# All products of probabilities with 128 columns, on eleven fixed tiles

## The chip, the cores and the metric

The kernel runs on one core of one Trainium2 chip. The metric is the device time of one execution in microseconds (us); it is a median over runs. Beside it stands one execution under the hardware profiler, with its own time and its trace. Engines are named as in the profile: PE (TensorE, matrix products), PEld (its weight loads, which run beside the products), DVE (VectorE), ACT (ScalarE), POOL (GpSimd) and SP (which issues most transfers).

## The reference

Three layers follow one another. First attention with a threshold, over 4 batches, 8 heads, 576 queries and keys and a head size of 64:

```python
scores = scale * np.matmul(q, k.transpose(0, 1, 3, 2))
thresh = np.max(scores, axis=-1, keepdims=True) - tau
scores = np.where(scores >= thresh, scores, -1000000000.0)
scores = scores - np.max(scores, axis=-1, keepdims=True)
attn = np.exp(scores)
attn = attn / (np.sum(attn, axis=-1, keepdims=True) + 1e-09)
return np.matmul(attn, v).astype(np.float32)
```

Its output, with the heads side by side, is a row of 512 values for each of 2304 tokens. Then each token goes through one of 8 experts (512 to 1024 and back, ReLU between); which one comes from the largest of its 8 logits, or from the token before it where a second gate says so. Last come a layer norm, a dense layer 512 to 2048 to 512 with ReLU, and a sum with its input. The change lies in attention.

## The kernel before, in words

**Attention.** The loop `while it < NI or later` goes over items. An item is (p, j): p is one of 16 pairs of heads (two heads of one batch), j one of 9 blocks of keys, in the order 8, 0, 1, ... 7. Blocks 0 to 3 are 128 keys each of the pair's first head, 4 to 7 those of the second, and block 8 has the last 64 keys of both, one head in each half of the partitions. Each turn of the loop works on several items at different stages:

- `s_mm` (PE) makes scores with queries on the partitions, and `mx` (DVE, L403) takes their maximum for each query, one item ahead of `s_mm` of the next. `th_parts` and `th_rows` turn a pair's maxima into rows of thresholds.
- `t_mm` (PE, L436 and L441) makes scores again with keys on the partitions, minus the thresholds; `ex` (ACT, L446) takes the exponential; `mask` (DVE, L452) sets to zero what lies below the threshold and writes tile `em`, of which there are two buffers.
- `hilo` splits the masked probabilities into two halves of 16 bits: ACT copies (L458), POOL subtracts (L459). Both go to a tile of 128 keys by 2 x 576 queries, `hl`, or `hlt` for block 8. `hl` has nine buffers in rotation, `hlt` two.
- `pv` (PE, L474 to L478) multiplies the halves with the values' halves, `vh` and `vl`. The probabilities are the weights (the stationary operand), so the queries are the columns of the array and the rows of the output `o`. A call makes one group of queries t of one head a: t from 0 to 3 has 128 queries, t = 4 has the last 64. It has fifteen products, three for each of five blocks of keys: high with `vh` (65 columns of output, the last one is the sum of the probabilities), high with `vl`, low with `vh`. For t = 4 the first of the three reads 128 columns of the tile all the same, so that all 128 rows of the output are written, and the other two read 64.
- `norm` (DVE, L489 to L493) divides by the sums after t = 4 of a head; then come the transfer to DRAM (`store`) and, from `gate`, transposes and the products for the routing.

Each engine works through its instructions in the order in which the loop issues them; `at` puts a step at a turn. `pv` of a pair's first head runs with its last group at turn 9p + 9, that of the second head at 9p + 13; `norm` follows one turn later, ahead of that turn's `mask`. Within a turn the order is: `mx`, `ex`, `mask`, `hilo`, the next `s_mm`, `pv`, `t_mm`, and then the rest (`gate` and `route` for tokens that are done, loads and splits of q, k and v for pairs to come, and the making of 16-bit halves of the dense layer's weights: `ffn_steps`, L142 to L164).

**Columns.** `columns(a, t)` gives the first column of a group: the first head's queries 0 to 511 are followed by its last 64 at 512, the second head's last 64 stand at column 0 of its tile, ahead of the others.

**After attention.** Experts, two tiles of 128 tokens each and then further tiles by counts; then the dense layer. Weights come in through SP's queue and are split on ACT and DVE. `blanks` writes constants once at the start.

Of the kernel before, what the change touches and what calls it, by code (L numbers as in the profile page):

```python
# [9 lines left out]
F16 = mybir.dt.float16  # L10
I32 = mybir.dt.int32
BF16 = mybir.dt.bfloat16
AF = mybir.ActivationFunctionType
ALU = mybir.AluOpType
# [6 lines left out]
def kernel(  # L21
# [15 lines left out]
    nc = tc.nc  # L37
# [15 lines left out]
    def pool(c, name, bufs, **kw):  # L53
        return c.enter_context(tc.tile_pool(name=name, bufs=bufs, **kw))
# [152 lines left out]
    R = dict(side="right")  # L207
    c_raw, c_tab, c_unit, c_tail, c_cv, c_pv, c_main = (ExitStack() for _ in range(7))
# [8 lines left out]
    cv_p = pool(c_cv, "cv", 2, **R)  # L217
    vb_p = pool(c_pv, "vb", 1, **R)
    sm_p = pool(c_pv, "sm", 2, **R)
    hl_p = pool(c_pv, "hl", 9, **R)  # L220
    ps_v = pool(c_pv, "ps_v", 1, space=PSUM, **R)
    em_p = pool(c_main, "em", 2, **R)
    e_p = pool(c_main, "e", 2, **R)
# [6 lines left out]
    if True:  # L230
# [15 lines left out]
        def blanks():  # L246
            V, G = nc.vector, nc.gpsimd
            for i in range(2):
                vh = vb[i][0]
                V.memset(pts[i], 0.0)  # L250
                G.memset(vh[:, :, 64:65], 16.0)
                G.memset(vh[64:128, 4, 64:65], 0.0)
                G.memset(vh[0:64, 5, 64:65], 0.0)
                V.memset(lgs[i], 0.0)
                V.memset(e1s[i], 0.0)
                V.memset(xts[i][:, 4, 64:128], 0.0)
                V.memset(mcs[i], 0.0)
            V.memset(erow, 0.0)
            V.memset(oh, 0.0)
            V.memset(one1, 1.0)  # L260
            V.tensor_copy(out=identb, in_=ident)
            V.memset(ind, 0.0)
            for i in range(4):
                V.memset(ind[32 * i:32 * i + 3, i, :], 1.0)
# [94 lines left out]
        def split_v(p):  # L359
# [2 lines left out]
            nc.scalar.activation(out=vh[:, :, 0:64], in_=r, func=AF.Copy)  # L362
            nc.gpsimd.tensor_tensor(out=vl, in0=r, in1=vh[:, :, 0:64], op=ALU.subtract)

        mms, mst, hls, ths, pvs, xcs = {}, {}, {}, {}, {}, {}
        W0 = 224
        mm = nc.tensor.matmul
# [11 lines left out]
        def columns(a, t):  # L379

            return 128 * t + 64 * a if t < 4 else 512 * (1 - a)
# [72 lines left out]

        def hilo(p, j):
            em = mst.pop((p, j))
            hl = hl_p.tile([128, 2, 576], F16, name="hlt" if j == 8 else "hl", bufs=2 if j == 8 else 9)
            nc.scalar.activation(out=hl[:, 0], in_=em, func=AF.Copy)  # L458
            nc.gpsimd.tensor_tensor(out=hl[:, 1], in0=em, in1=hl[:, 0], op=ALU.subtract)  # L459
            hls[p, j] = hl  # L460

        def pv(p, a, t):

            vh, vl = vb[p % 2]
            if t == 0:
                pvs[p, a] = ps_v.tile([128, 5, 100], F32, name="o")
            M = 128 if t < 4 else 64
            o, n = pvs[p, a][0:M, t], columns(a, t)
            for c in range(5):
                hl = hls[p, 4 * a + c if c < 4 else 8]  # L470
                jv = (c, 4)[c == 4] if a == 0 else (6 + c, 5)[c == 4]
                hi = hl.rearrange("p a b -> p (a b)")[:, n:n + 128]
                if c < 4:
                    mm(pvs[p, a][:, t, 0:65], hi, vh[:, jv, 0:65], start=(c == 0), stop=False)  # L474
                mm(o[:, 0:64], hl[:, 0, n:n + M], vl[:, jv, :], start=False, stop=False)
                mm(o[:, 0:65], hl[:, 1, n:n + M], vh[:, jv, 0:65], start=False, stop=False)
                if c == 4:
                    mm(pvs[p, a][:, t, 0:65], hi, vh[:, jv, 0:65], start=False, stop=True)  # L478
            if t == 4:
                for c in range(4):  # L480
                    del hls[p, 4 * a + c]
                if a: del hls[p, 8]
# [77 lines left out]
        def route(b):  # L560
# [112 lines left out]
            def f_A(t):  # L673
                for i in range(5):
                    M = 128 if i < 4 else 64
                    for a in range(2):
                        nc.tensor.matmul(t[:, 0:4 * E], ol[0:M, i], ov[0:M, i, 2 * a:2 * a + 2].rearrange("p a b -> p (a b)"), start=(i + a == 0), stop=(i + a == 5))

# [74 lines left out]
        for p in range(npair):  # L753
            if p:
                for lead, f, *a in soon.get(p, prep):
                    at(9 * p - lead, f, p, *a)
                at(9 * p - 4, th_parts, p)
                at(9 * p - 2, th_rows, p)
            for a in range(2):
                for n, ts in enumerate(((0, 1), (2, 3), (4,))):  # L760
                    for t in ts:
                        at(9 * p + 7 + 4 * a + n, pv, p, a, t)
                at(9 * p + 10 + 4 * a, start_norm, p, a)
            at(9 * p + 15 + (4 if p == npair - 2 else 1 if p < npair - 2 else 0), store, p)
            at(9 * p + (17 if p < npair - 1 else 15), lambda p=p: bgp.append(gate(p)))
# [109 lines left out]
    def dyn_tables():  # L875
        A = P["pa"].tile([128, 4, 128], F32, name="a").rearrange("p a b -> p (a b)")[:, 0:2 * NDYN]
        for i in range(B * 5):
            M = 128 if i % 5 < 4 else 64
            for a in range(2):
# [40 lines left out]
    for u in range(E + ND0):  # L920
        fq += [(u, j) for j in range(8)]
        n = 0 if u == 0 else 1
# [262 lines left out]
    with tc.manual_schedule():  # L1185
# [20 lines left out]
        for nm in "qkv":  # L1206
            load(0, nm, 1)
        blanks()
        nc.vector.tensor_scalar(out=ge, in0=t0, scalar1=0.0, scalar2=None, op0=ALU.is_ge)
        nc.vector.tensor_scalar(out=qs, in0=ge, scalar1=16.0, scalar2=None, op0=ALU.mult)  # L1210
# [14 lines left out]
        while it < NI or later:  # L1225
# [13 lines left out]
            if 0 < it <= NI: hilo(*items[it - 1])  # L1239
# [3 lines left out]
            for f, a in todo:  # L1243
                if f in (pv, th_rows): f(*a)
# [3 lines left out]
            for f, a in todo:  # L1248
                if f not in (pv, th_rows, start_norm): f(*a)
# [44 lines left out]
        while bgp:  # L1294
            n = len(bgp)
# [112 lines left out]
```

## Time and profile before

| what | us |
|---|---|
| median of 3 runs | 1051.86 |
| lowest and highest of them | 1051.25, 1055.43 |
| the profiled execution, its own time | 1051.45 |
| its span, first to last instruction | 1049.7 |
| PE busy in the span | 990.2 |
| DVE busy | 652.8 |
| ACT busy | 505.1 |
| POOL busy | 392.8 |

The span lies inside the profiled execution's time. A busy time is a sum over stages with different limits, so the shares of the whole span say little of one stage. Idle time of an engine costs something only where another engine waits for it. The granted clock of PE is 1.00 for full speed; the mean over this span is 0.988.

### The profile page before, as it was taken

What the parts mean: (1) busy time and instruction counts of PE and PEld (TensorE: products, weight loads), DVE (VectorE), ACT (ScalarE), POOL (GpSimd) and SP (SyncE); (2) the same over time, 40 slices, a digit from 0 to 9 for tenths busy, and PEclk for the clock granted to TensorE, in tenths of its full rate; (3) what the DMA queues carried; (4) which work ended last, traced back from release to release, by engine and by line L of the source; (5) the groups of instructions that cost most, each with busy time, mean ns of one, the idle gap of its engine ahead of it and who ended that gap; (6) DMA issues with size and microseconds to landing.
All of it is one profiled execution on the core that took longest, in us unless ns stands there. A gap on an engine that the chain in (4) does not pass through costs nothing. (4 is left out here: it accounts for less than half of the span.)

```text
span 1049.7 us, 23757 instructions
## 1 busy us (share of the span) xinstructions
PE 990.2 (94%) x9946; PEld 728.9 (69%) x9946; DVE 652.8 (62%) x1127; ACT 505.1 (48%) x791; POOL 392.8 (37%) x411
## 2 busy tenths in 40 slices
PE   6899998998999988899999999999999999999995
PEld 3678877787888776676667677594858668567572
DVE  7788888988897777797787777363324133131220
ACT  4688786786777666356566554242212011011010
POOL 3699897797788671334222211101000000000000
PEclk8999999999999999999999999999999999999998
DMA  7556544464442646668889775363111110111100
GB/s 179 138 133 166 132 103 126 112 156 119 113 108 47 166 153 213 214 217 278 268 290 304 239 251 164 105 200 106 38 31 40 52 32 31 54 28 41 31 11 23
DMA packets 122454, 136.83 MB, mean 130 GB/s; under 512 B 65370, under 2 KB 86874, under 8 KB 122336
## 3 DMA queue, kind: packets, MB, share of 16 engines
q1 hardware_dynamic: 98336, 116.43, 38.3%
q0 software_dynamic: 4960, 14.17, 3.7%
q10 hardware_dynamic: 19040, 4.61, 2.1%
q8 instruction: 80, 1.31, 0.5%
q14 instruction: 38, 0.31, 0.1%
HBM read 100.17 MB, written 19.94 MB: 114 GB/s over the span
## 5 line engine op out<-in xcount | busy, mean ns | idle before, releaser
L1144 PE MATMUL a<-nT,fw 128*128 128x256 f16 x1728 | 190.3, 273 | 0.8 <-DVE nT L1113 0.8
L459 POOL TENSOR_TENSOR hl<-em,hl 128x576 f16<-128x576 f32 x128 | 169.5, 1325 | 54.0 <-ACT hl L458 52.8
L1157 PE MATMUL y<-fw,hid 128*128 128x512 f16 x864 | 187.9, 379 | 0.0
L1144 PEld LDWEIGHTS <-fw 128*128 128x128 f16 x1728 | 169.1, 98 | 22.4 <-issue 0.9
L1157 PEld LDWEIGHTS <-hid 128*128 128x128 f16 x864 | 84.6, 98 | 100.4
L1147 ACT ACTIVATE hid<-a 128x512 f16<-128x512 f32 x72 | 42.7, 593 | 213.2 <-PE a L1144 211.3
L125 DVE SCALAR_TENSOR_TENSOR w<-stg,w 128x1024 f16<-128x1024 f32 x112 | 135.2, 1231 | 15.7 <-ACT w L124 14.8
L446 ACT ACTIVATE e<-s,t 128x576 f32<-128x576 f32 x144 | 106.0, 736 | 70.2 <-PE s L441 57.6
L1162 POOL DMA_INDIRECT out_dram<-xf x18 | 19.1, 1059 | 311.8 <-DVE xf L1161 311.8
L1012 PE MATMUL a<-xT,w 128*128 128x128 f16 (+1 forms) x1536 | 121.4, 241 | 1.4 <-DVE w L125 0.9
L1033 PE MATMUL y<-w,hid 128*128 128x512 f16 x528 | 117.8, 379 | 3.0 <-DVE hid L1017 2.7
L1012 PEld LDWEIGHTS <-w 128*128 128x128 f16 x1536 | 112.2, 99 | 11.1 <-DVE w L125 1.0
L403 DVE TENSOR_REDUCE mc<-sm 128x1 f32<-128x576 f32 x138 | 103.6, 751 | 24.7 <-PE sm L399 22.7
L124 ACT ACTIVATE w<-stg 128x1024 f16<-128x1024 f32 x112 | 114.4, 1051 | 6.1 <-DMA stg<-in_moe_w_dram 3.5
L452 DVE SCALAR_TENSOR_TENSOR em<-s,e 128x576 f32<-128x576 f32 x144 | 107.1, 745 | 9.7 <-POOL hl L459 8.5
L1148 DVE SCALAR_TENSOR_TENSOR hid<-a,hid 128x512 f16<-128x512 f32 x72 | 49.6, 688 | 98.9 <-ACT hid L1147 98.9
L1161 DVE SCALAR_TENSOR_TENSOR xf<-y,xf 128x512 f32<-128x512 f32 x18 | 12.5, 692 | 146.8 <-PE y L1157 146.8
L399 PE MATMUL sm<-qkt 128*128 128x288 f16 (+1 forms) x308 | 75.4, 291 | 24.3 <-DVE mc L403 21.4
L458 ACT ACTIVATE hl<-em 128x576 f16<-128x576 f32 x128 | 86.9, 679 | 18.8 <-DVE em L452 18.3
L1033 PEld LDWEIGHTS <-hid 128*128 128x128 f16 x528 | 51.0, 98 | 62.2 <-DVE hid L1017 4.5
L436 PE MATMUL s<-qkt 128*128 128x288 f16 (+1 forms) x320 | 90.2, 290 | 3.8 <-DVE em L452 3.1
L441 PE MATMUL s<-th,ind 128*128 128x128 bf16 (+5 forms) x960 | 91.9, 206 | 0.0
(295 smaller groups left out, 1800.4 us busy)
## 6 DMA issues: line engine op xcount, KB each, us to landing
stg<-in_moe_w_dram SPq DMA_DIRECT2D x112, 512.0 KB
stg<-in_moe_w_ch_dram SPq DMA_DIRECT2D x32, 512.0 KB
ys_d<-stg SPq DMA_DIRECT2D x6, 769.5 KB
xf<-ys_d SPq DMA_DIRECT2D x9, 513.0 KB
x_d<-xc SPq DMA_DIRECT2D x16, 256.0 KB
ku<-qkt SPq DMA_DIRECT2D x28, 144.0 KB
rawq<-in_q_dram SPq DMA_DIRECT2D x7, 512.0 KB
rawk<-in_k_dram SPq DMA_DIRECT2D x7, 512.0 KB
```

The source lines that it names most:

```text
L124: nc.scalar.activation(out=dst[:, 0, n], in_=t, func=AF.Copy, scale=scale)
L125: nc.vector.scalar_tensor_tensor(out=dst[:, 1, n], in0=t, scalar=scale, in1=dst[:, 0, n], op0=ALU.mult, op1=ALU.subtract)
L403: nc.vector.tensor_reduce(out=mcs[p % 2][:, j:j + 1], in_=mms.pop((p, j))[:, W0:W0 + 576], op=ALU.max, axis=AX.X)
L436: mm(o[:, W0 + 288 * c:W0 + 288 * c + 288], (kt, ku)[k][:, n], y, start=(k == 0), stop=False)
L441: mm(o[:, W0 + i:W0 + i + w], ind[:, t % 4, 0:o.shape[0]], y, start=False, stop=(i == of[-1][0]))
L446: nc.scalar.activation(out=e, in_=mst[p, j][:, W0:W0 + 576], func=AF.Exp, bias=t0, scale=SC)
L452: nc.vector.scalar_tensor_tensor(out=em, in0=ps[:, W0:W0 + 576], scalar=0.0, in1=e, op0=ALU.is_ge, op1=ALU.mult)
L459: nc.gpsimd.tensor_tensor(out=hl[:, 1], in0=em, in1=hl[:, 0], op=ALU.subtract)
L1012: nc.tensor.matmul(ps[:, f, :], t1[:, a, c, fc], x[:, h, i:i + N // 128, c, :], start=(n == 0), stop=(n == 11))
L1033: nc.tensor.matmul(ps, hid[:, x, f, 128 * i:128 * i + 128], t2[:, a, f, :], start=(n == 0), stop=(n == 23))
L1144: nc.tensor.matmul(ps[:, f, :], fw1[:, a, c, fc], x[:, h, :, c, :], start=(n == 0), stop=(n == 11))
L1157: nc.tensor.matmul(ps, hid[:, x, f, ts_], fw2[:, a, f, :], start=(n == 0), stop=(n == 47))
```

## The change

For the last 64 queries of a head every product now reads 128 columns of the tile and writes 128 rows of the output. The 64 rows more are not used. For the second head, whose last queries stand at column 0, the columns beside them are the next 64 queries. For the first head they are, in the high half, the first 64 columns of the low half, and in the low half 64 columns of zeros, which the tile gets behind it. For this the tiles are made once, eleven of them, with a row of 2 x 576 + 64 values; POOL writes the zeros at the start. Block (p, j) uses tile (8p + j) mod 9, and block 8 uses tile 9 + p mod 2. In the last block of keys the product of high with `vh` comes first, as in the others.

```diff
-    hl_p = pool(c_pv, "hl", 9, **R)
+    hl_p = pool(c_pv, "hl", 1, **R)
...
+            for hl in hlt:
+                G.memset(hl[:, 1152:1216], 0.0)
...
+        hlt = [hl_p.tile([128, 2 * 576 + 64], F16, name=f"hl{i}") for i in range(11)]
...
-            hl = hl_p.tile([128, 2, 576], F16, name="hlt" if j == 8 else "hl", bufs=2 if j == 8 else 9)
-            nc.scalar.activation(out=hl[:, 0], in_=em, func=AF.Copy)
-            nc.gpsimd.tensor_tensor(out=hl[:, 1], in0=em, in1=hl[:, 0], op=ALU.subtract)
+            hl = hlt[9 + p % 2] if j == 8 else hlt[(8 * p + j) % 9]
+            nc.scalar.activation(out=hl[:, 0:576], in_=em, func=AF.Copy)
+            nc.gpsimd.tensor_tensor(out=hl[:, 576:1152], in0=em, in1=hl[:, 0:576], op=ALU.subtract)
...
-            M = 128 if t < 4 else 64
-            o, n = pvs[p, a][0:M, t], columns(a, t)
+            o, n = pvs[p, a][:, t], columns(a, t)
             for c in range(5):
                 hl = hls[p, 4 * a + c if c < 4 else 8]
                 jv = (c, 4)[c == 4] if a == 0 else (6 + c, 5)[c == 4]
-                hi = hl.rearrange("p a b -> p (a b)")[:, n:n + 128]
-                if c < 4:
-                    mm(pvs[p, a][:, t, 0:65], hi, vh[:, jv, 0:65], start=(c == 0), stop=False)
-                mm(o[:, 0:64], hl[:, 0, n:n + M], vl[:, jv, :], start=False, stop=False)
-                mm(o[:, 0:65], hl[:, 1, n:n + M], vh[:, jv, 0:65], start=False, stop=False)
-                if c == 4:
-                    mm(pvs[p, a][:, t, 0:65], hi, vh[:, jv, 0:65], start=False, stop=True)
+                hi, lo = hl[:, n:n + 128], hl[:, 576 + n:704 + n]
+                mm(o[:, 0:65], hi, vh[:, jv, 0:65], start=(c == 0), stop=False)
+                mm(o[:, 0:64], hi, vl[:, jv, :], start=False, stop=False)
+                mm(o[:, 0:65], lo, vh[:, jv, 0:65], start=False, stop=(c == 4))
```

## Rows read from the trace of the kernel before

**Rows 1.** Busy time by stage (window: length, then each engine, PE's clock, DMA).

```profile
core 0: us, PE busy (x) PEld busy (x) DVE busy (x) ACT busy (x) POOL busy (x), PEclk, DMA share, GB/s
...
47.00:402.00 355.00, 333.14 (x4889) 278.09 (x4886) 302.06 (x543) 265.52 (x447) 285.96 (x276) 1.00 0.49 125
402.00:1049.70 647.70, 625.12 (x4828) 430.39 (x4825) 314.83 (x509) 215.54 (x309) 85.32 (x82) 0.99 0.41 130
```

**Rows 2.** Busy time of single pairs of heads in the loop, same columns.

```profile
87.24:109.33 22.09, 21.58 (x318) 18.05 (x315) 19.40 (x32) 18.22 (x32) 20.11 (x19) 1.00 0.53 133
153.51:180.36 26.85, 22.42 (x322) 18.50 (x319) 23.28 (x48) 18.62 (x33) 19.25 (x19) 1.00 0.47 124
180.36:203.80 23.44, 22.15 (x331) 18.64 (x329) 21.28 (x42) 16.44 (x28) 16.82 (x17) 1.00 0.40 103
247.99:275.64 27.65, 23.56 (x322) 19.47 (x320) 23.18 (x48) 18.33 (x33) 19.16 (x19) 0.94 0.44 120
...
321.14:343.01 21.87, 21.39 (x318) 18.01 (x316) 17.61 (x29) 17.10 (x30) 18.42 (x19) 1.00 0.26 55
```

**Rows 3.** Waits of DVE, 47 to 402 us (in total, times, longest).

```profile
DVE rd L489 <- PE o L478: 23.8, 30, 2.4
DVE mc L403 <- PE sm L399: 14.7, 20, 2.0
DVE em L452 <- POOL hl L459: 8.5, 13, 1.9
```

**Rows 4.** Weight loads of the products of probabilities by shape (busy us, mean ns).

```profile
L474 PEld LDWEIGHTS <-hl 128*128 128x128 f16 x640 | 60.6, 98 | 9.1 <-issue 2.9
...
L475 PEld LDWEIGHTS <-hl 128*64 128x64 f16 x128 | 13.6, 106 | 6.9
```

**Rows 5.** Timeline of PE, a block of 128 queries and what follows (start, duration).

```profile
194.29 0.19 PE L474 MATMUL o<-vh,hl 128*128 128x65 f16 x1
194.32 0.19 PE L475 MATMUL o<-vl,hl 128*128 128x64 f16 x1
...
194.74 0.19 PE L474 MATMUL o<-vh,hl 128*128 128x65 f16 x1
```

**Rows 6.** Timeline of PE, a first head's block of the last 64 queries.

```profile
212.79 0.19 PE L474 MATMUL o<-vh,hl 128*128 128x65 f16 x1
212.92 0.22 PE L475 MATMUL o<-vl,hl 128*64 128x64 f16 x1
...
213.10 0.20 PE L474 MATMUL o<-vh,hl 128*128 128x65 f16 x1
...
214.15 0.29 PE L436 MATMUL s<-qkt 128*128 128x288 f16 x1
```

**Rows 7.** Timeline of DVE at three such blocks (last column: idle before).

```profile
190.91 0.17 DVE L489 TENSOR_SCALAR rd<-o 128x5 f32<-128x5 f32 x1 [0.42 <-PE o L478]
...
201.26 0.16 DVE L489 TENSOR_SCALAR rd<-o 128x5 f32<-128x5 f32 x1 [0.70 <-PE o L478]
...
214.35 0.17 DVE L489 TENSOR_SCALAR rd<-o 128x5 f32<-128x5 f32 x1 [0.60 <-PE o L478]
...
216.42 0.76 DVE L452 SCALAR_TENSOR_TENSOR em<-s,e 128x576 f32<-128x576 f32 x1
```

**Rows 8.** Timeline of POOL, 203 to 219 us.

```profile
203.80 1.29 POOL L459 TENSOR_TENSOR hl<-em,hl 128x576 f16<-128x576 f32 x1 [2.05 <-ACT hl L458]
...
215.11 1.27 POOL L459 TENSOR_TENSOR hl<-em,hl 128x576 f16<-128x576 f32 x1
216.56 1.28 POOL L459 TENSOR_TENSOR hlt<-em,hlt 128x576 f16<-128x576 f32 x1 [0.17 <-ACT hlt L458]
```

**Rows 9.** Timeline of POOL at the start.

```profile
0.74 0.20 POOL masks.py:197 MEMSET ident<- 128x128 f32 x1 [0.29 <-POOLq L1392]
...
1.26 0.14 POOL L251 MEMSET vh<- 128x10 f16 x1
...
9.59 1.27 POOL L306 TENSOR_TENSOR nat<-rawq,nat 128x576 f16<-128x576 f32 x1 [3.37 <-ACT nat L305]
```

**Rows 10.** The instructions of line L146 (min, median and max ns).

```profile
L146 DVE SCALAR_TENSOR_TENSOR cv<-stg,cv x22: 681/692/1659, 41.6 to 327.2; 128x512 int32<-128x512 int32 x22
```

## The prediction

> **What bounds the kernel now.** I read the granted clock and the page's slices first, then busy time by stage, then waits, then the timelines of single blocks. By stage [rows 1]: the attention loop runs from 47 to 402 us with PE busy 333 of 355 us, the experts and the dense layer fill the rest with PE busy 625 of 648 us. The change touches products of the attention loop alone; what follows has no clock of its own, since its loads are issued in program order as buffers come free, so what the loop saves should arrive whole at the end.
>
> Inside the loop a pair of heads takes about 22.1 us where nothing else disturbs it [rows 2] (the row of 87.24; eight pairs look like it, the last of them the row of 321.14): PE 21.58 busy, POOL 20.11, DVE 19.40. PE is nearly full, POOL is only 2 us behind. So it is not enough to count what PE saves; I must see what is late next.
>
> The waits say where PE holds the others up [rows 3]: DVE's largest wait is the first step of the norm, L489, for the last product of probabilities, L478: 23.8 us in 30 waits. The norm follows exactly the block of products for a head's last 64 queries.
>
> **The products.** A block for 128 queries, fifteen products, goes from 194.29 to 194.74: 0.45 us, one product each 0.03 us [rows 5]. The block for the last 64 queries has the same fifteen, ten of them with 64 columns. It goes from 212.79 to 214.15: 1.36 us [rows 6]. The steps inside say why: the first product has 128 columns, the next starts 0.13 us later with 64, and a group of three takes 0.31 us (212.79 to 213.10) where three equal products take 0.09. PE pays at each change between 64 and 128 columns, twice in each group. After the change all fifteen have 128 columns and the block should take the 0.45 us of its neighbours: 0.91 us less. There are 32 such blocks (128 loads of this kind over four a block [rows 4]), so PE gets back 32 x 0.91 = 29.1 us. The bounds for a block are 0 (if the cost came from somewhere else than the change of columns) and 0.91; I take 0.91, as the block of rows 5 is the new block in every respect: same tiles, same columns, same order but for the last three.
>
> Against the change speaks that ten weight loads grow from 64 to 128 columns. In the trace 64 columns took 106 ns and 128 columns 98 [rows 4], so the smaller load buys nothing, and I charge nothing. The Trainium skill (TensorE: Matmul & The Clock Gate, LDWEIGHTS) says that a load's time goes by its columns, 128 ones at 1.2 columns a ns. By that rule ten loads would cost an estimated 53 ns more each, a block would save 0.38 us instead of 0.91, and the sum below would be about 10 us and the time about 1041, at the slow end of my forecast's own range. The durations of this trace do not bear it out, and I give it 0.02 of the forecast's chance.
>
> **What of the 0.91 us reaches the end.** DVE is the engine to follow, because PE's next scores wait for its maxima. In a second head's block DVE has finished a maximum and stands 0.70 us until the norm can start, at 201.26 [rows 7]. With the block 0.91 us shorter this wait is gone and then DVE's own maximum comes last: gain 0.70 us, not 0.91. POOL does not stand in the way there: it stood idle 2.05 us before the step at 203.80 [rows 8]. Behind the norm stand, on DVE, the mask, then the copy on ACT, then POOL's subtraction: all of them come 0.70 us earlier. Fifteen blocks (after the sixteenth, DVE has splits of expert weights ahead of the norm): 15 x 0.70 = 10.5 us.
>
> A first head's block ends differently. DVE waits 0.60 us for the norm, at 214.35 [rows 7], but POOL has been working without a break since 203.80, until the subtraction that ends at 215.11 + 1.27 = 216.38 [rows 8]. The mask at 216.42 [rows 7] needs one of two buffers, and it is that subtraction which frees it. So the 0.60 us turns into a wait for POOL; what remains is the 0.17 us that POOL idles before its next step. In eight pairs it is like that: 8 x 0.17 = 1.4 us. In the other eight POOL is less busy (16.82 of 23.44 us, the row of 180.36 [rows 2]), there the same wait is 0.42 us, at 190.91 [rows 7], and I take it whole: 8 x 0.42 = 3.4 us.
>
> Sum: 10.5 + 1.4 + 3.4 = 15.3 us.
>
> **The tiles and the zeros.** Eleven fixed tiles take the place of eleven rotating buffers with the same order of use: nine for the first kind, two for the other. A buffer comes back after nine tiles, when its last products are at least three steps of the loop old, and in the waits of ACT this copy never waits for PE. I charge nothing; if that cover were gone a copy would wait for one block, 0.45 us. A product of the last 64 queries now reads 64 columns more, the low half's included; the product that leads each group read that far already, so it waits for nothing new. Eleven memsets of 64 values are added on POOL at the start: 0.14 us for 10 values, 0.20 us for 128 [rows 9], so 1.5 to 2.2 us. POOL idles 3.37 us before its first subtraction at 9.59 [rows 9], since ACT's copy is not there; that hides them. Without this cover they would cost at most 2.2 us.
>
> The profiled execution took 1051.45 us, 0.41 below the median of the runs (1051.86), well inside their spread. 1051.45 - 15.3 = 1036.2 us.
>
> **The rivals.** *All of PE's saving comes back.* 1051.45 - 29.1 = 1022.3 us. For it: PE is busy 21.58 of 22.09 us in a pair [rows 2], and the wait for the norm alone is 23.8 us [rows 3]. Against it: DVE's maximum ends 0.70 us before the norm, so nothing can start 0.91 us earlier, and POOL's run bars the first head. Between 1022 and 1031: chance 0.20.
>
> *POOL and DVE get into each other's way and take the gain.* The same DVE step, L146, takes 0.69 us in the median and 1.66 at most [rows 10]; the long ones lie where POOL works without a break. A pair where small DVE steps fall on such a run takes 26.85 us instead of 23.44 [rows 2] (rows of 153.51 and 180.36). With POOL at 20.11 us of a pair of some 21.3, such meetings get likelier. If every one of 14 pairs has one long step more, 14 x 0.97 = 13.6 us are lost again and 1.7 stay: 1049.8 us. Against it: in the eight like pairs POOL and DVE are moved by the same amount, so their meetings stay what they are. Between 1042 and 1051: chance 0.25, half of it above 1046. The Trainium skill (SBUF — State Buffer, Who interferes with whom) says that DVE and GpSimd share one pair of ports, held for a whole instruction, and that the other blocks; the long L146 fit that.
>
> *The clock falls, and it gets slower.* PE has more idle time in each pair, and around 256 us the granted clock fell once after a long idle stretch: the pair of 247.99 had 0.94 and took 27.65 us, its twin of 153.51 had 1.00 and 26.85 [rows 2]. One fall costs 0.80 us. To lose the 15.3 us and 5.3 more, it would have to fall some 26 times, nearly twice in each pair. Chance 0.03: the idle stretches shown follow DVE's long runs, not these blocks, and the change shortens the busy part, it does not lengthen an idle one by more than a few tenths.
>
> That the change does nothing (the 1.36 us not being due to the columns) would leave 1051; I count it in the second rival.
>
> **How the numbers follow.** Forecast, between 1031 and 1042: 0.52; more: 0.20; less: 0.25; slower: 0.03. A measurement of this kernel can tell about 0.5% (5.3 us) from no change, so faster begins below 1046.2: 0.52 + 0.20 + 0.12 = 0.84; same 0.12; slower 0.04. The range goes from 1027 to 1046.5: it leaves out a quarter of the second case, less than half of the third and the slower one, together about 0.19.
>
> **What would show it.** In the changed kernel's trace: no product of probabilities with 64 columns; the block of the last queries at 0.45 us; DVE's wait for it near zero; pairs of 21.2 to 21.4 us in the loop, with POOL's idle time near nothing and DVE waiting for POOL more than the trace of before shows. Pairs of 20.5 us or less would prove the POOL step wrong: then something else than POOL held the first head's block. A block that still takes over 0.6 us would prove the reading of the columns wrong, and long DVE steps in more pairs the second rival right.

## The result, and the profile after

The median of four runs is 1038.94 us after the change (1038.51 to 1040.08) and 1052.34 us before it (four runs, 1051.25 to 1055.43). The ratio is 0.987, with a 95% interval from 0.9857 to 0.9883: 13.4 us less. The forecast was 1036.2 us, 2.7 us below the median and inside its range of 1027 to 1046.5. The profiled execution took 1038.88 us, against 1051.45 before: 12.6 us less where the sum had 15.3.

Windows of the changed kernel: the two stages (the attention loop, then the rest), then a pair of heads that nothing else disturbs, cut where those of [rows 2] are. Columns as in [rows 1].

```profile
47.00:402.00 355.00, 314.70 (x4975) 269.03 (x4970) 315.56 (x567) 273.84 (x457) 288.08 (x275) 0.99 0.52 135
402.00:1037.10 635.10, 615.52 (x4719) 421.79 (x4718) 305.05 (x485) 207.92 (x298) 84.58 (x82) 0.99 0.40 128
106.88:128.07 21.19, 19.85 (x318) 16.99 (x315) 19.38 (x32) 18.29 (x32) 20.36 (x20) 1.00 0.69 163
```

Seven of the eight such pairs now take 20.9 to 21.2 us where most took 22.09 [rows 2]; the other, from 63.81 us, still takes 22.08, with PE waiting 0.9 us for a transfer in it. PE, nearly full before, is idle 1.34 us of the pair shown; POOL has become the busiest engine, idle only 0.83 us of it.

Two pairs did not get shorter: those in which DVE has the later steps of a routing to do. The first of them, cut at the start of the same two masks, so that DVE's instructions are the same in both windows, in the kernel before and in the changed one:

```profile
166.11:188.74 22.63, 22.25 (x324) 18.58 (x324) 18.59 (x41) 17.23 (x30) 17.32 (x19) 1.00 0.40 107
162.11:184.97 22.86, 20.61 (x324) 17.51 (x324) 20.77 (x41) 17.36 (x30) 18.05 (x19) 1.00 0.45 119
```

Its twin went from 23.53 to 23.81 us. PE is relieved, but DVE is busy 2.2 us longer: three small routing steps take 1.22, 1.00 and 0.88 us where they took 0.2 each. The timelines show one of them in the changed kernel, POOL's subtraction beside it, and the same step in the kernel before.

```profile
180.65 1.22 DVE L644 TENSOR_TENSOR rk<-rk,oh 128x40 f32<-128x40 f32 x1
180.54 1.28 POOL L462 TENSOR_TENSOR hl<-em,hl 128x576 f16<-128x576 f32 x1
185.46 0.19 DVE L645 TENSOR_TENSOR rk<-rk,oh 128x40 f32<-128x40 f32 x1
```

Started 0.11 us after the subtraction, the step ends 0.05 us after it.

DVE's waits in the changed kernel, 47 to 402 us (in total, times, longest).

```profile
DVE mc L406 <- PE sm L402: 18.6, 19, 2.1
DVE em L455 <- POOL hl L462: 7.8, 15, 1.4
DVE rd L488 <- PE o L477: 4.9, 3, 2.2
```

The wait for the last product of probabilities has gone from 23.8 us in 30 waits [rows 3] to 4.9 us in 3. Another wait has grown instead: the same view gives for PE's scores waiting for DVE's maxima 25.0 us, against 16.5 before.

PE's timeline in the changed kernel, the block for a second head's last 64 queries and what follows it (start, duration).

```profile
116.51 0.19 PE L475 MATMUL o<-vh,hl 128*128 128x65 f16 x1
116.54 0.20 PE L476 MATMUL o<-vl,hl 128*128 128x64 f16 x1
116.57 0.19 PE L477 MATMUL o<-vh,hl 128*128 128x65 f16 x1
...
116.96 0.29 PE L439 MATMUL s<-qkt 128*128 128x288 f16 x1
```

116.51 to 116.96 is 0.45 us, as in [rows 5] and not the 1.36 us of [rows 6]. The weight loads did not become dearer (groups of loads by shape, whole span; busy us, mean ns):

```profile
L475 PEld LDWEIGHTS <-hl 128*128 128x128 f16 x800 | 74.1, 97 | 5.7 <-issue 2.9 <-DVE xc L492 0.6
```

How much of the time is gained inside the loop, the list of one line's instructions shows. The loop's masks, in the changed kernel:

```profile
L455 DVE SCALAR_TENSOR_TENSOR em<-s,e x144: 729/742/759, 30.2 to 380.4; 128x576 f32<-128x576 f32 x144
```

The last mask starts at 380.4 us, where the same view of the kernel before has 392.5: 12.1 of the 12.6 us are gained up to there.

### The profile page after: what moved, and what is told of

Its sections match the earlier page's. It is cut to its first block, busy times and chain, and to the rows that moved or that the text cites. A ratio compares the mean times of both kernels' runs of the same rounds, so it can differ in the third digit from the quotient of the medians.

```text
span 1037.1 us, 23768 instructions
## 1 busy us (share of the span) xinstructions
PE 962.8 (93%) x9946; PEld 711.7 (69%) x9946; DVE 656.1 (63%) x1127; ACT 506.5 (49%) x791; POOL 396.4 (38%) x422
## 5 line engine op out<-in xcount | busy, mean ns | idle before, releaser
L462 POOL TENSOR_TENSOR hl<-em,hl 128x576 f16<-128x576 f32 x144 | 192.9, 1343 | 56.1 <-ACT hl L461 53.2
L461 ACT ACTIVATE hl<-em 128x576 f16<-128x576 f32 x144 | 97.8, 679 | 23.4 <-DVE em L455 22.8
```

The source lines that it names most:

```text
L461: nc.scalar.activation(out=hl[:, 0:576], in_=em, func=AF.Copy)
L462: nc.gpsimd.tensor_tensor(out=hl[:, 576:1152], in0=em, in1=hl[:, 0:576], op=ALU.subtract)
```

## The experiments

Each kernel ran beside the kernel before on the same chip; a ratio is to that one, with its 95% interval. "A like pair" is a pair of heads that nothing else disturbs, 22.09 us before and mostly 20.9 to 21.2 after.

**Only the tiles and the zeros.** The ten products with 64 columns stay, in the old order.

```diff
+                M = 128 if t < 4 else 64
+                if c < 4:
+                    mm(o[:, 0:65], hi, vh[:, jv, 0:65], start=(c == 0), stop=False)
+                mm(o[0:M, 0:64], hl[:, n:n + M], vl[:, jv, :], start=False, stop=False)
+                mm(o[0:M, 0:65], hl[:, 576 + n:576 + n + M], vh[:, jv, 0:65], start=False, stop=False)
+                if c == 4:
+                    mm(o[:, 0:65], hi, vh[:, jv, 0:65], start=False, stop=True)
```

> The eleven fixed tiles, their zeros and the memsets alone; the products of the last 64 queries keep 64 columns. If the gain comes from the columns: within 2 us of the kernel before, and the blocks of the last queries still take 1.36 us. If part of the gain comes from the fixed tiles (other waits at the copy, the start of the loop 0.6 us earlier): 1 to 6 us faster than before.

1052.11 us against 1052.00, ratio 0.9999 (0.9979 to 1.0019); a like pair takes 22.09 us. Tiles and zeros neither cost nor give anything, as far as an interval of 2 us either way can tell.

**128 columns only for the second heads, or only for the first.** The edit is shown against the kernel with the tiles alone.

```diff
-                M = 128 if t < 4 else 64
+                M = 128 if t < 4 or a == 1 else 64
```

and with `a == 0` in the other kernel.

> 128 columns for the second head's last queries alone, the first head's keep 64. By the forecast's sum this block brings 0.70 us, fifteen times: 10.5 us of the gain, so about 1041 to 1042 us. If PE's time alone counted, half of the whole gain of 13.4 us: 1045 to 1046 us.

> 128 columns for the first head's last queries alone. By the forecast's sum 1.4 + 3.4 = 4.8 us, so about 1047 us, with DVE's wait at the norm of the first head gone and a wait of the mask for POOL in its place. If PE's time alone counted, half of the whole gain: 1045 to 1046 us. If POOL held the block fully: 1050 us or more.

Second heads alone: 1046.01 us, ratio 0.9947 (0.9927 to 0.9967), 5.6 us (3.5 to 7.7) where the forecast's term was 10.5. First heads alone: 1045.96 us, 0.9939 (0.9916 to 0.9963), 6.4 us (3.9 to 8.8) where the terms were 4.8 together. The two add up to 12.0, close to the 13.4 of the whole.

In the kernel with the second heads alone, DVE's waits for the last product (47 to 402 us) fell as foreseen, from 23.8 to 13.1 us: 10.7, where the term says 10.5.

```profile
DVE rd L492 <- PE o L481: 13.1, 17, 2.4
DVE em L455 <- POOL hl L462: 4.1, 5, 1.4
```

But DVE's own work got longer. Its line L146, a step in the making of the dense layer's weights, in the list of that line's instructions (min, median, max ns), in this kernel:

```profile
L146 DVE SCALAR_TENSOR_TENSOR cv<-stg,cv x22: 681/1316/1724, 41.3 to 324.2; 128x512 int32<-128x512 int32 x22
```

The median is 1316 ns, 692 before [rows 10]. Before the change the step began 1.2 us after POOL's step L158, once that was over (at 108.48 and 107.30 us, for one). DVE's timeline of this kernel in one like pair shows it right behind a norm that no longer waits:

```profile
105.53 0.15 DVE L492 TENSOR_SCALAR rd<-o 128x5 f32<-128x5 f32 x1
...
106.87 1.31 DVE L146 SCALAR_TENSOR_TENSOR cv<-stg,cv 128x512 int32<-128x512 int32 x1
```

and POOL's timeline of the same kernel shows what is running beside it, with L158 begun only 0.4 us earlier:

```profile
106.47 1.16 POOL L158 TENSOR_TENSOR fw<-cv,fw 128x512 f16<-128x512 f32 x1
107.59 1.72 POOL L462 TENSOR_TENSOR hl<-em,hl 128x576 f16<-128x576 f32 x1
```

Two of POOL's steps that read memory run during L146, and the second of them takes 1.72 us instead of 1.28. In the busy times by line, 47 to 402 us, DVE's steps L142, L144 and L146 took 58.6 us together before and take 64.3 here, 5.7 more. A like pair takes 21.84 us, though a few take less: 0.25 us gained, not 0.70. In this pair DVE waits 0.7 us less for the last product and 0.4 less for POOL, but it works 0.46 us longer and waits 0.5 longer for PE's scores.

More is lost in the two pairs with the later routing steps. The first of them, cut as above:

```profile
163.98:187.73 23.75, 21.50 (x324) 18.00 (x324) 20.89 (x42) 17.37 (x29) 18.04 (x19) 1.00 0.50 136
```

It took 22.63 us before, its twin 23.53 and now 24.87: 1.1 and 1.3 us lost where 0.70 each had been counted as won. That is 3.9 of the 4.9 us by which the term was too large. The Trainium skill (SBUF — State Buffer, Who interferes with whom) says that a DVE instruction with two inputs in SBUF contends with a GpSimd instruction that reads SBUF; L146 has two inputs and fits that, and so does the routing step on `rk`.

With the first heads alone a like pair takes 21.90 us, 0.19 less, where the forecast had 0.17, and DVE waits more for POOL (8.5 us in 13 waits before [rows 3]):

```profile
DVE em L455 <- POOL hl L462: 12.0, 21, 1.7
```

Here the 0.60 us did turn into a wait for POOL, as the forecast said.

**64 columns kept, but all ten such products in a row.** Two changes of the columns in a block instead of eight: the order of the products before the change gives eight, not the nine of the expectation. `part(c)` gives the tile of block c and the index of its values.

```diff
...
+            if t == 4:
+                for c in range(4):
+                    hl, jv = part(c)
+                    mm(o[:, 0:65], hl[:, n:n + 128], vh[:, jv, 0:65], start=(c == 0), stop=False)
+                for c in range(5):
+                    hl, jv = part(c)
+                    mm(o[0:64, 0:64], hl[:, n:n + 64], vl[:, jv, :], start=False, stop=False)
+                    mm(o[0:64, 0:65], hl[:, 576 + n:640 + n], vh[:, jv, 0:65], start=False, stop=False)
+                hl, jv = part(4)
+                mm(o[:, 0:65], hl[:, n:n + 128], vh[:, jv, 0:65], start=False, stop=True)
...
```

> Fixed tiles, 64 columns kept, but the ten products with 64 columns of a block stand together: two changes of columns in a block and not nine. If the change of columns costs, a block takes 0.65 to 0.75 us and 10 to 13 us come back, about 1040 us. If a product with 64 columns is slow by itself, the block stays above 1.2 us and the time near 1052 us.

1039.49 us, ratio 0.989 (0.9862 to 0.9919), as good as the changed kernel within what can be told. PE's timeline of this kernel, one block:

```profile
115.91 0.29 PE L477 MATMUL o<-vh,hl 128*128 128x65 f16 x4
116.13 0.22 PE L480 MATMUL o<-vl,hl 128*64 128x64 f16 x1
116.19 0.20 PE L481 MATMUL o<-vh,hl 128*64 128x65 f16 x1
116.22 0.20 PE L480 MATMUL o<-vl,hl 128*64 128x64 f16 x1
...
116.44 0.20 PE L481 MATMUL o<-vh,hl 128*64 128x65 f16 x1
116.57 0.20 PE L483 MATMUL o<-vh,hl 128*128 128x65 f16 x1
116.61 0.29 PE L439 MATMUL s<-qkt 128*128 128x288 f16 x1
```

The block takes 0.70 us. Inside the row of ten a product of 64 columns follows the last one after about 0.03 us, like one of 128; only going from 64 back to 128 (116.44 to 116.57) takes 0.13. So what was dear is the change and not the narrow product. With 0.25 us for two changes (0.70 - 0.45), the eight changes of the old block come to 1.0 us; 0.91 was measured, 0.11 each. The Trainium skill (TensorEngine Tiling (Array Packing), Key Properties) says that changing the tiling mode drains TensorE; the trace fits that and puts about 0.1 us on a change, but shows no drain as such.

**The new block three times over.** 45 products of 128 columns take the place of fifteen. The first two passes are computed and thrown away.

```diff
-            for c in range(5):
+            for c in [0, 1, 2, 3, 4] * (3 if t == 4 else 1):
```

> The changed kernel, but the block of the last queries is made three times over, each time anew (same result): 45 products of 128 columns, about 1.36 us, as long as the block before the change, with no change of columns in it. If only the time that PE spends on the block counts: back to 1051 to 1053 us. If the changes of columns also cost outside of the block (later products, other engines): it stays 3 us or more below the kernel before.

1052.39 us, ratio 0.9994 (0.9972 to 1.0017). PE's timeline of this kernel, one such block and what follows:

```profile
106.77 0.20 PE L475 MATMUL o<-vh,hl 128*128 128x65 f16 x1
...
108.11 0.19 PE L477 MATMUL o<-vh,hl 128*128 128x65 f16 x1
108.14 0.29 PE L439 MATMUL s<-qkt 128*128 128x288 f16 x1
```

The block takes 1.37 us, as the old one did, and a window over a like pair is that of [rows 2] again:

```profile
88.87:110.96 22.09, 21.58 (x374) 18.81 (x374) 19.40 (x32) 18.24 (x32) 20.10 (x20) 1.00 0.51 133
```

With PE's time put back and no 64-column product left, the kernel is where it was. So the gain comes from PE's time in these blocks; nothing else of the change gives more than the interval's 2 to 3 us.

**Less work for POOL.** In two more kernels, the one before and the changed one, the low halves of the dense layer's weights are zeros, written by a memset (22 pieces), and not the difference; that part of the output is left out.

```diff
-            nc.gpsimd.tensor_tensor(out=dst[:, 1, a], in0=rf, in1=dst[:, 0, a], op=ALU.subtract)
+            nc.gpsimd.memset(dst[:, 1, a], 0.0)
```

> The kernel before with the same zeros in place of the 22 low halves. There the blocks of the last queries set the pairs as well as POOL, so a lighter POOL should bring little: at most 3 us. If POOL set the pairs of the kernel before already, as much as in the changed kernel: 6 to 12 us.

> The changed kernel, but POOL writes zeros instead of the low halves of the dense layer's weights that it makes inside the attention loop (22 pieces; these low halves are left out). A subtraction of 1.16 us becomes a memset of some 0.3 us, twice in a pair. If POOL's run sets the pairs of the changed kernel: pairs of 20.3 to 20.9 us instead of 21.5, 6 to 12 us faster than the changed kernel. If DVE or PE sets them: at most 2 us.

On the kernel before: 1052.62 us, ratio 0.9994 (0.9978 to 1.0011). On the changed kernel: 1029.39 us, 0.978 (0.9739 to 0.982): 23.6 us below the kernel before, against 13.4 with POOL's work in full. A window over a like pair of the first (before, lighter), columns as in [rows 1]:

```profile
88.59:110.68 22.09, 21.57 (x314) 18.06 (x314) 19.40 (x33) 18.24 (x32) 18.81 (x20) 1.00 0.52 133
```

and of the second (after, lighter):

```profile
95.15:115.79 20.64, 19.85 (x318) 17.00 (x315) 19.25 (x32) 18.14 (x32) 18.86 (x20) 1.00 0.61 121
```

POOL's busy time is the same in both, 18.8 us. Before the change the pair stays at 22.09 with PE full; after it the pair falls to 20.64, though the one right behind it takes 21.47. So POOL holds the changed kernel and did not hold the kernel before.

POOL can hold a kernel by the amount of its work or by its meetings with DVE, and this edit lessens both: a memset takes 0.52 us instead of 1.16, and it reads nothing. In this second kernel the median of L146 is back at 687 ns; at 103.48 us, for one, it takes 0.68, most of it in a gap of 0.62 us in which POOL stands idle. And the first pair with the later routing steps, cut as above, takes

```profile
158.91:179.75 20.84, 20.43 (x324) 17.52 (x324) 18.37 (x41) 16.99 (x30) 16.17 (x18) 1.00 0.42 115
```

where the changed kernel has 22.86. POOL was idle 4.8 us of that, so its amount of work was not what held this pair; DVE's three small steps are back at 0.2 us each. With the twin (20.84 instead of 23.81, there behind a fall of the clock that this execution doesn't have) these two pairs make 5.0 of the about 10 us.

**A third buffer for the masked probabilities,** on the changed kernel.

```diff
-    em_p = pool(c_main, "em", 2, **R)
+    em_p = pool(c_main, "em", 3, **R)
```

> The changed kernel with three buffers for the masked probabilities instead of two, so that a mask does not wait for POOL's subtraction of two blocks before. If POOL's amount of work sets the pairs: at most 2 us faster, POOL only falls behind. If only the two buffers tie DVE to POOL: 4 to 8 us faster.

1039.20 us, ratio 0.9863 (0.9824 to 0.9901): no gain over the changed kernel. Masks waited 7.8 us for POOL in the changed kernel; with three buffers that wait is not in the list any more, so it was the buffer they waited for. In its place DVE's L142, L144 and L146 take 65.5 us instead of 59.0, with this kernel's L146 at

```profile
L146 DVE SCALAR_TENSOR_TENSOR cv<-stg,cv x22: 681/1460/1658, 42.0 to 320.8; 128x512 int32<-128x512 int32 x22
```

The wait went, and longer steps stand in its place.

**Without L146 for half of the weight pieces.** The last three bits of these weights are left out; on the changed kernel and on the one before.

```diff
-        for _ in range(3):
-            yield next(n)
+        for i in range(3):
+            yield next(n) if i < 2 or a else None
```

> The changed kernel without the third DVE step (L146) of half of the pieces of the dense layer's weights, eleven steps; it leaves out the last three bits of these weights. In the changed kernel this step lies on POOL's subtraction one turn after the second head's block and takes 1.31 us instead of 0.68, and the subtraction 1.72 instead of 1.28. If that meeting eats the second head's gain: 4 to 6 us faster than the changed kernel, 1033 to 1035 us. If POOL's own work sets the pairs and the meeting only fills idle time: 0 to 2 us, 1037 to 1039 us.

> The kernel before without the same eleven steps (the last three bits of these weights are left out). There the step lies in an idle stretch of POOL, takes 0.68 us, and DVE then waits for PE's scores anyway. By both theories at most 1.5 us faster than before; more would mean that the step costs as such and the run beside it says nothing of a meeting.

On the kernel before: 1054.22 us, ratio 1.0009 (0.9989 to 1.003). On the changed one: 1038.43 us, 0.986 (0.983 to 0.989). Windows over a like pair and over the first half of a pair with routing steps, of the latter kernel:

```profile
96.97:117.97 21.00, 19.82 (x318) 16.99 (x315) 18.72 (x31) 18.36 (x32) 20.09 (x20) 1.00 0.60 119
148.82:166.59 17.77, 13.51 (x169) 11.16 (x169) 15.27 (x29) 10.84 (x20) 11.67 (x13) 0.81 0.69 179
```

The changed kernel has 21.30 and 14.89 us at these places, both at a clock of 1.00. So this like pair gains 0.30 us; cut at the start of the same masks, four like pairs that took 21.2 us take 20.99, 21.33, 20.99 and 20.89. From the loop's first mask to the second of these places 3.0 us are gained, and then 2.9 are lost in that one half pair, in which the granted clock is 0.81. PE's timeline there:

```profile
157.60 0.40 PE L402 MATMUL sm<-qkt 128*128 128x288 f16 x1 [3.11 <-DVE mc L406]
```

PE had stood idle 3.11 us for a maximum, behind small routing steps on DVE of 1.2 us each, and the clock was 0.50, the lower level of 1.2 GHz, from 157 to 162 us. The meeting of L146 with POOL costs 0.2 to 0.3 us in three of these four; taking half of the steps away bought nothing in the end, and in this execution the clock took back what was won.

**POOL's work given to DVE.** First the low halves of v, then the five small steps of the thresholds, each on the changed kernel.

```diff
-            nc.gpsimd.tensor_tensor(out=vl, in0=r, in1=vh[:, :, 0:64], op=ALU.subtract)
+            nc.vector.tensor_tensor(out=vl, in0=r, in1=vh[:, :, 0:64], op=ALU.subtract)
```

```diff
-            G = nc.gpsimd if p else nc.vector
+            G = nc.vector
```

> The changed kernel with the low half of the values made on DVE instead of POOL: POOL loses a step of 1.79 us in each pair's long run, DVE gets one of about 0.75. If POOL's run sets the pairs of the changed kernel: 6 to 12 us faster than the changed kernel. If DVE sets them: same or slower.

> The changed kernel with the five small steps of the thresholds on DVE instead of POOL in every pair: POOL loses about 1.4 us in its long run, DVE gets about 0.9. If POOL's run sets the pairs: 4 to 10 us faster than the changed kernel. If DVE sets them: the same or up to 10 us slower.

1073.93 us, ratio 1.0199 (1.0169 to 1.023), and 1070.98 us, 1.0169 (1.0129 to 1.021): 35 and 32 us above the changed kernel. DVE's timeline with the low halves of v:

```profile
118.14 0.74 DVE L455 SCALAR_TENSOR_TENSOR em<-s,e 128x576 f32<-128x576 f32 x1
121.52 1.32 DVE L365 TENSOR_TENSOR vl<-vraw,vh 128x640 f16<-128x640 f32 x1 [2.63 <-ACT vh L364]
122.76 0.74 DVE L406 TENSOR_REDUCE mc<-sm 128x1 f32<-128x576 f32 x1
```

The subtraction reaches DVE's queue before ACT has made the high halves, and the maximum of the next scores stands behind it: 42.6 us in 15 such waits, more than the 35 us lost, and the step takes 1.32 us where 0.75 was expected. A lighter POOL can't show beside that, so the kernel says nothing on POOL. With the thresholds on DVE a window over the loop shows POOL relieved but PE slower:

```profile
47.00:420.00 373.00, 325.85 (x4891) 276.93 (x4891) 311.93 (x616) 270.15 (x449) 263.85 (x206) 0.93 0.46 118
```

PE waits 37.9 us for DVE's maxima (25.0 in the changed kernel) and its clock is 0.93 in the loop. At most 10 us more had been expected; how much of the 32 us is the wait and how much the clock these runs don't separate.

## Why the prediction was right, and where its terms were off

**The products.** Right. The block went from 1.36 to 0.45 us. That the cost lay in the changes of columns is shown by the kernel that keeps 64 columns and groups them, and that PE's time is the cause by the one with 45 products.

**The loads, the tiles, the zeros.** Right: loads of 97 ns, and no time for tiles and zeros alone. All eleven memsets took 0.97 us, the estimate was 1.5 to 2.2; POOL still idled 2.38 us before its first subtraction.

**The whole saving arrives at the end.** Right: 12.1 us at the loop's last mask, 12.6 at the end.

**The second heads' term, 15 x 0.70 = 10.5 us.** Mis-sized: 5.6 us measured alone, and 10.5 is outside the interval. The step that failed is "all of them come 0.70 us earlier". The wait did go (10.7 us of it), but what stands behind the norm on DVE is not only mask, copy and subtraction: L146 came earlier too, and in two pairs the small routing steps, and they met POOL's subtractions and grew. This is the second rival's mechanism. Against it the forecast had said of the like pairs that "POOL and DVE are moved by the same amount, so their meetings stay what they are"; they were not, for L146 now starts 0.4 us behind POOL's L158 instead of 1.2.

In the changed kernel the like pairs came out nearly as foreseen (0.9 us less in most, where 0.70 + 0.17 had been counted), though L146 has grown there too. It is the two pairs with the later routing steps that failed: 0.70 + 0.42 less had been counted for each, and they took 0.23 and 0.28 us more. That makes 2.7 us, as much as the profiled execution fell short of the sum (12.6 of 15.3). That the two agree so well is partly luck: other pairs were off too, one of them by 0.9 us.

**The first heads' terms, 1.4 + 3.4 = 4.8 us.** Held: 6.4 us (3.9 to 8.8), with 0.19 us in a like pair where 0.17 was foreseen, and the wait turned into one for POOL.

**POOL is late next.** Right: the same relief of POOL gives nothing that can be told before the change and about 10 us after it. It is also where the rest of PE's 29.1 us went: with POOL lighter, 23.6 of them come back. The sign given in advance was half wrong: POOL's idle time did shrink, to 0.8 us of a pair, but masks wait for it no more than before in sum (7.8 us, 8.5 in [rows 3]). The load shows as longer DVE steps and as PE waiting for maxima as well, and a third buffer only moves it from one to the other. That POOL holds the changed kernel is shown; how much of it by its amount of work and how much by its meetings with DVE is not, save that in the two pairs with the later routing steps it is the meetings.

**The other rivals.** That all comes back would have been 1022.3 us; it fails for POOL. The clock did not fall more often: the mean is 0.987, 0.988 before. The two experiments where it fell more show that the rival's mechanism exists, but the change itself doesn't lengthen PE's longest waits (2.7 us at most for a maximum, 3.1 before).

## What to carry to other kernels

On PE count the changes of the array's columns, not the columns: mixing tiles of 64 and 128 cost more than computing 64 useless columns, and grouping them was as good as widening them, within what can be told. Before booking such a saving, ask which engine is second: here POOL was 2 us behind in a pair of 22; of 29 us 16 did not arrive, and 10 of these came when POOL had less to do and met DVE less. A step that comes earlier on one engine takes all its queue along, and what it then runs beside can be dearer than the wait that it lost.

## What was unexpected of the hardware

A weight-making step of DVE (L146) takes 0.69 us with POOL idle and 1.3 to 1.7 us beside POOL's subtractions, and those grow from 1.28 to 1.72 us: both sides lose. A routing step on 40 values in each partition can stand for a whole subtraction: 0.19 us became 1.22.

PE's clock did not answer alike to like idle times. In the changed kernel two waits for a maximum are almost equal (PE's timeline):

```profile
158.43 0.28 PE L402 MATMUL sm<-qkt 128*128 128x288 f16 x1 [2.66 <-DVE mc L406]
...
249.97 0.40 PE L402 MATMUL sm<-qkt 128*128 128x288 f16 x1 [2.67 <-DVE mc L406]
```

After the first the product takes its usual 0.28 us, after the second 0.40: there the clock had fallen. What tells the two apart these runs don't show.
